# Windowed attention in a fused mixing kernel: the sums over v in eight tiles of 64 keys by 32 columns instead of four of 128 by 32, with two PSUM banks and an add on VectorE

## The chip, the cores and the metric

The kernel runs on one core of one Trainium2 chip. Its five engines are called by their short names in the profile: PE (TensorE, with PEld for its weight loads), DVE (VectorE), ACT (ScalarE), POOL (GpSimd) and SP (SyncE, which here only issues DMAs). The metric is the device time of one execution in microseconds; the time of a kernel is the median of its runs.

## The reference

All arrays are float32. `x` is 2048 tokens by 512 features. The output is a gated sum of two branches over the same `x`:

```
g = sigmoid((x * gate_w).sum(-1))
# branch A: Fourier mixing, the real part of a 2-D DFT, as four matrix products
a, b = x @ dft_hid_re.T, x @ dft_hid_im.T
A = dft_seq_re @ a - dft_seq_im @ b
# branch B: attention, 32 heads of 16 columns, causal, window of 256 keys
q, k, v = split(x @ wqkv)
scores = (q @ k.T) * 16 ** -0.5
scores = where(0 <= i - j < 256, scores, -1e9)
B = softmax(scores) @ v @ wo
out = g * A + (1 - g) * B
```

The change is in `softmax(scores) @ v`.

## The kernel before

Most of the work on PE is dense: the projections to q, k and v, the two hidden DFTs and the two sequence DFTs. Each float32 operand of a dense product is split into a high and a low part, and three products of the parts are summed. In the trace these are the tiles `d` (line 527, in two row halves of 64 partitions that run at the same time, `64*128`) and `dc` and `d` of lines 580 and 567 (whole array, `128*128`). The function `halves64` yields them step by step; a step is one matmul for the upper and one for the lower half.

The attention runs beside the dense work. The 32 heads are 8 groups of 4 heads, and the 2048 keys are 16 blocks of 128. The main loop (at the end of `fnet_window_mix`) counts `n` over 128 (group, key block) pairs, and each `n` has four quarter steps `q`. In quarters 0 and 2 stands `s_pair` (line 363, scores of 128 queries against up to 384 keys, two heads in the two row halves; DVE then takes the masked minimum, line 367). In quarters 1 and 3 stands `t_pair` (line 422, the same scores with keys on the partitions, for the pair nine blocks earlier; ACT takes the exponential into `pt`, line 425, and POOL zeroes the corners of the window, lines 427 and 431). After each of these `fill` puts in a few dense steps, as many as keep the dense work evenly spread. The whole order on PE, ACT, DVE, POOL and SP is written out by the program, and each engine works in that order.

Once for every 512 queries of a group, 32 times in all, `pv` (line 445) makes the sums of v. Call these the 32 blocks, numbered from 0; block `i` is group `i // 4` and quarter `c = i % 4` of the queries. It stands after quarter 3, behind the fill, so that the next instructions on PE are `s_pair`, fill, `t_pair`. For each key block it multiplies `pt` (128 keys by up to 384 queries) with the 32 columns of v of one head, and the four heads `j` take the four column tiles of the array (`128*32` in the trace). Column 16 of each 32 holds ones, so row 16 of a result is the sum of the weights. A quarter with `c > 0` takes six key blocks (1, 2, 3, 3, 2 and 1 blocks of 128 queries: 1536 columns for each head), a first quarter takes four (3, 3, 2, 1: 1152 columns). The operands are plain float32, and the trace has two matmuls, with two weight loads, for each one in the program.

The results of `s_pair`, `t_pair` and `pv` share a pool of PSUM, `ps_a`, with two buffers of two banks each. They go round: in 28 of the 32 blocks `pv` takes one buffer, the next `s_pair` the other, and the `t_pair` after it the buffer of `pv` again, for which ACT must have copied the sums out. (After block 27 that `t_pair` takes the other buffer, and the last three blocks have no `s_pair` behind them.) `pv` itself uses one bank of its buffer.

What follows a block is set off at fixed distances in quarter steps (the list `far`, line 1108): `o_evict` (line 454, ACT copies the 128 by 512 sums into one of three places of `ots`) after 1, `l_move` (the small DMA `lt<-ots` of the rows with the sums of weights, from SP's queue) after 4, then the reciprocal on DVE, its round trip through DRAM, and `o_mul` (line 475, POOL multiplies the sums by the reciprocals) after 28, and the store `o_scr<-ev` after 32. The next block comes 16 quarter steps after this one.

Of the kernel before, what the change touches and what calls it, by code (L numbers as in the profile page):

```python
# [7 lines left out]
F32 = mybir.dt.float32  # L8
# [6 lines left out]
P = 128  # L15
# [4 lines left out]
HG = 4  # L20
GROUPS = 8
NB = S // P
# [22 lines left out]
def fnet_window_mix(ctx: ExitStack, tc: tile.TileContext, xT, x, wqk, wv, wr, wi, cr, ci, wo, gw, out):  # L45
    nc = tc.nc
# [3 lines left out]
    st = ctx.enter_context(tc.tile_pool(name="st", bufs=4))  # L50
    ev = ctx.enter_context(tc.tile_pool(name="ev", bufs=EV))
    at = ctx.enter_context(tc.tile_pool(name="at", bufs=2))
    ps_a = ctx.enter_context(tc.tile_pool(name="ps_a", bufs=2, space=PSUM))
# [12 lines left out]
    def ld(dst, src):  # L66
        mark("sp", nc.sync.dma_start(dst, src))
# [11 lines left out]
    def mark(e, ins):  # L79
        last[e] = ins.ins  # L80
# [108 lines left out]
    with tc.manual_schedule(engines={mybir.EngineType.Activation, mybir.EngineType.DVE, mybir.EngineType.SP}):  # L189
# [11 lines left out]
        for dk in range(DK):  # L201
            c = slice(dk * 256, dk * 256 + 256)
# [29 lines left out]
    vt = [const.tile([P, 4, P], F32, name=f"vt{b}") for b in range(3)]  # L232
# [166 lines left out]
    PT = {}  # L399
# [34 lines left out]
    OT = {}  # L434
    ots = const.tile([P, 3, 512], F32, name="ots", tag="pt7")

    def pv(i):
        G, c = divmod(i, 4)
        o = ps_a.tile([P, 2, 512], F32, name="o", tag="st")[:, 0]
        kbs = range(max(0, 4 * c - 2), 4 * c + 4)  # L440
        for kb in kbs:
            a, e = max(kb, 4 * c), min(kb + 2, 4 * c + 3) + 1
            v = vt[(4 * G + kb // 4) % 3]
            for j in range(HG):
                nc.tensor.matmul(o[32 * j:32 * j + 32, (a - 4 * c) * P:(e - 4 * c) * P],  # L445
                                 v[:, kb % 4, 32 * j:32 * j + 32],
                                 PT[G * NB + kb][:, j, (a - kb) * P:(e - kb) * P],
                                 start=kb == kbs[0], stop=kb == kbs[-1], skip_group_check=True)
        OT[i] = o

    def o_evict(i):
        o = OT[i]
        OT[i] = ots[:, i % 3]
        nc.scalar.copy(OT[i], o)

    LT = {}

    def l_move(i):
        LT[i] = at.tile([P, 16], F32, name="lt")
        ld(LT[i], ots[:, i % 3][16:P:32])  # L460

    def l_turn(i):
        nc.vector.reciprocal(LT[i], LT[i])
# [625 lines left out]
    def at_time(t, fn, *args):  # L1089
        agenda.setdefault(t, []).append((fn, args))  # L1090
# [14 lines left out]
    for i in range(4 * GROUPS):  # L1105
        t = 4 * (VISIT * i + VISIT + LAG) + 3
        at_time(t + 0.5, pv, i)
        far = (1, 3, 9, 11, 16, 21, 24) if i == 4 * GROUPS - 1 else (1, 4, 11, 15, 21, 28, 32)
        for d, fn in zip(far, (o_evict, l_move, l_turn, l_inv, l_back, o_mul, o_out)):
            at_time(t + d, fn, i)  # L1110
        if i:
            at_time(t + 2, v_next, i + 2)
            at_time(t + 12, v_spread, i + 2)
# [73 lines left out]
```

## Time and profile before

| | |
|---|---|
| median of 3 runs | 849.21 us (847.05 to 849.4) |
| profiled execution, its own time | 850.56 us |
| its span | 848.9 us |
| mean granted clock of TensorE | 0.996 |
| PE busy | 821.5 us, 97% of the span |
| DVE, ACT, POOL busy | 63%, 49%, 43% |

A row of the groups by line reads: line, engine, operation, the tiles it writes and reads, shapes and count, then busy time in us (overlaps counted once) and the mean length of one in ns, then the idle time of its engine just before and what ended it. Matmuls overlap in the array, so the mean length of one is longer than the distance from one to the next. A row of the timeline has start and length in us, then engine, line and tiles; neighbours of one kind are merged into one row with a count.

### The profile page before, as it was taken

The page shows a single profiled execution, that of the slowest core. Times are in us where ns is not written, and L with a number is a line of the kernel's source. Part 1 is how long each engine was busy: PE and PEld are TensorE (multiplying, and loading weights), DVE is VectorE, ACT ScalarE, POOL GpSimd, SP SyncE. Part 2 cuts the span into 40 slices and gives each one's busy share as a digit, 9 for nine tenths or more (in the row PEclk, how much of TensorE's full clock was granted, in tenths as well). Part 3 has the DMA queues.
Part 4 walks back from the last instruction along what each step waited for, and adds up shares of the span by engine and source line. Part 5 has one row for each costly group of instructions (what it writes and reads, how often), then busy time and mean ns, then how long its engine had stood idle before and what let it go on. Part 6 is the DMA issues. An engine that isn't in the chain of part 4 may idle for free.

```text
span 848.9 us, 19774 instructions
## 1 busy us (share of the span) xinstructions
PE 821.5 (97%) x7298; PEld 654.2 (77%) x7298; DVE 531.1 (63%) x1504; ACT 418.0 (49%) x814; POOL 365.0 (43%) x683
## 2 busy tenths in 40 slices
PE   9999999998999899999999999899999999999998
PEld 7898777777777687777777777777777778788886
DVE  7276765555666678666657656676877536555553
ACT  6234655455555556555655656455555645222320
POOL 5002344433334336444444444454543546674540
PEclk9999999999999999999999999999999999999999
DMA  9865875558977546455646566787785567865531
GB/s 341 279 207 163 283 247 182 169 181 261 302 263 211 144 124 197 138 175 155 169 142 181 153 192 187 226 231 228 237 230 184 168 180 224 261 213 190 179 111 50
DMA packets 109344, 168.80 MB, mean 199 GB/s; under 512 B 34240, under 2 KB 43968, under 8 KB 109248
## 3 DMA queue, kind: packets, MB, share of 16 engines
q1 hardware_dynamic: 96192, 127.04, 48.4%
q0 software_dynamic: 11088, 39.33, 15.4%
q10 hardware_dynamic: 1968, 1.18, 0.5%
q8 instruction: 57, 0.93, 0.5%
q14 instruction: 39, 0.32, 0.1%
HBM read 107.74 MB, written 59.51 MB: 197 GB/s over the span
## 4 chain that ended last, share of the span: by engine, by line
PE 76%; DMA 8%; DVE 7%; issue 5%; ACT 3%; POOL 1%; SPq 1%; ACTq 0%; DVEq 0%; POOLq 0%
PE d L527 41%; PE o L445 9%; PE dc L580 8%; PE s L363 6%; PE t L1012 5%; PE t L422 4%; DVE junk L367 3%; PE d L567 3%; DMA ring<-qk_scr 2%; DMA raw<-ci 2%; ACT pt L425 1%; DVE lo L156 1%; DMA o_scr<-ev 1%; DVE big L140 1%; DMA stage<-ab_scr 1%
## 5 line engine op out<-in xcount | busy, mean ns | idle before, releaser
L367 DVE CUSTOM_DVE_ANT_0 junk<-s,mask 128x384 f32<-128x384 f32 (+2 forms) x512 | 271.9, 531 | 198.0 <-PE s L363 186.9
L527 PE MATMUL d<-big,hi 64*128 64x512 f32 x1920 | 344.5, 394 | 0.0
L427 POOL TENSOR_SCALAR_AFFINE_SELECT pt<-pt 128x256 f32<-128x256 f32 x256 | 112.3, 439 | 359.4 <-ACT pt L425 280.8
L425 ACT ACTIVATE pt<-t 128x768 f32<-128x768 f32 (+2 forms) x256 | 197.6, 772 | 123.8 <-PE t L422 121.4
L527 PEld LDWEIGHTS d<-big,hi 64*128 64x128 f32 x1920 | 195.5, 187 | 27.0 <-issue 0.6
L527 PE MATMUL d<-big,lo 64*128 64x512 f32 x960 | 206.2, 395 | 0.0
L527 PE MATMUL d<-hi,big 64*128 64x512 f32 x672 | 132.3, 392 | 0.0
L363 PE MATMUL s<-ring,ring 48*128 48x384 f32 (+2 forms) x512 | 99.5, 357 | 12.4 <-DMA ring<-qk_scr 3.7
L527 PEld LDWEIGHTS d<-big,lo 64*128 64x128 f32 x960 | 100.6, 187 | 13.2 <-issue 0.2
L155 ACT CAST hi<-raw 128x512 fp32r<-128x512 f32 x142 | 87.1, 618 | 30.0 <-PE d L527 15.2
L156 DVE TENSOR_TENSOR lo<-raw,hi 128x512 fp32r<-128x512 f32 x110 | 85.4, 777 | 12.9 <-ACT hi L155 12.9
L431 POOL TENSOR_SCALAR_AFFINE_SELECT pt<-pt 128x256 f32<-128x256 f32 x224 | 92.9, 415 | 0.0
L580 PE MATMUL dc<-big,hi 128*128 128x512 f32 x284 | 91.7, 392 | 0.0
L422 PE MATMUL t<-ring,ring 50*128 50x384 f32 (+2 forms) x512 | 87.8, 330 | 1.0 <-ACT pt L425 0.5
L445 PE MATMUL o<-pt,vt 128*32 128x384 f32 (+2 forms) x1408 | 84.3, 386 | 3.9 <-DVE ml L367 3.7
L527 PEld LDWEIGHTS d<-hi,big 64*128 64x128 f32 x672 | 76.8, 186 | 7.4
L363 PEld LDWEIGHTS s<-ring,ring 48*128 48x128 f32 x512 | 53.7, 185 | 37.3 <-issue 10.4
L527 PE MATMUL d<-lo,big 64*128 64x512 f32 x336 | 80.4, 392 | 0.0
L445 PEld LDWEIGHTS o<-pt,vt 128*32 128x32 f32 x1408 | 42.0, 110 | 49.7 <-issue 27.6
L422 PEld LDWEIGHTS t<-ring,ring 50*128 50x128 f32 x512 | 50.7, 185 | 14.5 <-ACT pt L425 2.1
L156 POOL TENSOR_TENSOR lo<-raw,hi 128x512 fp32r<-128x512 f32 x32 | 43.0, 1356 | 40.8 <-ACT hi L155 40.5
L580 PEld LDWEIGHTS dc<-big,hi 128*128 128x128 f32 x284 | 52.3, 188 | 8.7 <-issue 0.2
(123 smaller groups left out, 858.3 us busy)
## 6 DMA issues: line engine op xcount, KB each, us to landing
ring<-qk_scr SPq DMA_DIRECT2D x128, 192.0 KB
qk_scr<-home SPq DMA_DIRECT2D x32, 512.0 KB
raw<-cr POOLq DMA_DIRECT2D x32, 512.0 KB, 5.6
r_scr<-ev SPq DMA_DIRECT2D x44, 256.0 KB
raw<-ci POOLq DMA_DIRECT2D x18, 512.0 KB, 5.7
qk_scr<-home SPq DMA_DIRECT2D x32, 256.0 KB
ev<-l_scr SPq DMA_DIRECT2D x32, 256.0 KB
o_scr<-ev SPq DMA_DIRECT2D x32, 256.0 KB
```

The costliest lines, as they stand in the source:

```text
L155: jobs.append(lambda c=c: nc.scalar.copy(hi[:, c], raw[:, c]))
L156: jobs.append(lambda c=c: (nc.gpsimd if FIN else nc.vector).tensor_sub(lo[:, c], raw[:, c], f(hi[:, c])))
L363: nc.tensor.matmul(ps[:, h, :w], ring[0][r, p, j * P:j * P + P], ring[1][r, p, k0:k0 + w], start=True, stop=True)
L367: mark("dve", nc.vector.tensor_tensor_reduce(out=junk[:, :w], in0=ps[:, h, :w], in1=mask[:, WIN - w:], scale=1.0, scalar=3e38, op0=OP.add, ...
L422: nc.tensor.matmul(ps[:, h, :w], ring[1][r, p, q0:q0 + P], ring[0][r, p, q0:q0 + w], start=True, stop=True)
L425: nc.scalar.activation(pt[:, ph, :w], ps[:, :, :w], AF.Exp, scale=-1.0)
L427: nc.gpsimd.affine_select(a, a, pattern=[[0, 2], [1, P]], compare_op=OP.is_ge, fill=0.0, base=0, channel_multiplier=-1)
L431: nc.gpsimd.affine_select(a, a, pattern=[[0, 2], [-1, P]], compare_op=OP.is_gt, fill=0.0, base=0, channel_multiplier=1)
L445: nc.tensor.matmul(o[32 * j:32 * j + 32, (a - 4 * c) * P:(e - 4 * c) * P], v[:, kb % 4, 32 * j:32 * j + 32], PT[G * NB + kb][:, j, (a - kb ...
L527: nc.tensor.matmul(o.ps, lhs[r], rhs[r], start=start, stop=end and o.left == 0, skip_group_check=True)
L580: nc.tensor.matmul(ps, w[a][:, i % 8 * 128:i % 8 * 128 + 128], ab[SC[i]][:, b], start=i == ends[0] and a + b == 0, stop=i == ends[1] and a ...
L1012: nc.tensor.matmul(ps, o[:, a, c], fin(n, b, c), start=start and c == 0 and a + b == 0, stop=c == 1 and a == 1, skip_group_check=True)
```

## The change

`pv` now cuts each key block of 128 into its two halves of 64 keys. A half block of keys can only be seen by its own 320 queries, so its matmul is at most 320 columns long, and it is cut further at the edges of the quarter. The lower and the upper 64 partitions of the array work as two row tiles, so there are eight tiles of 64 by 32: two halves times four heads. Sums of the lower half go to the first bank of the buffer, those of the upper half to the second. The half blocks are put in pairs, one from each half, of equal length where that can be: for `c > 0` six pairs of 320, 320, 256, 192, 128 and 64 columns, 1280 in all; for a first quarter 320 with 384, 320 with 320, 256 with 192 and 128 with 64, which is 1024 columns in the lower and 960 in the upper half. The program has 1408 such matmuls in place of 704.

`o_evict` copies both banks (128 by 1024) with one ACT instruction: into place 0 or 1 of `ots` by the parity of the block, and into place 2. A new step `o_add`, two quarter steps after the block, adds place 2 to place 0 or 1 on DVE. `l_move` reads the added place. The rest of the chain keeps its distances.

```
-        o = ps_a.tile([P, 2, 512], F32, name="o", tag="st")[:, 0]
+        o = ps_a.tile([P, 2, 512], F32, name="o", tag="st")
...
-                nc.tensor.matmul(o[32 * j:32 * j + 32, (a - 4 * c) * P:(e - 4 * c) * P],
-                                 v[:, kb % 4, 32 * j:32 * j + 32],
-                                 PT[G * NB + kb][:, j, (a - kb) * P:(e - kb) * P],
-                                 start=kb == kbs[0], stop=kb == kbs[-1], skip_group_check=True)
+                spans[kb, h] = 0 if kb == 0 else max(k0, q0), min(k0 + 320, q0 + 512)
...
+        for n, pair in enumerate(pairs):
+            for h, (kb, _) in enumerate(pair):
+                a, e = spans[kb, h]
+                r = slice(64 * h, 64 * h + 64)
+                v = vt[(4 * G + kb // 4) % 3]
+                for j in range(HG):
+                    nc.tensor.matmul(o[32 * j:32 * j + 32, h, a - q0:e - q0], v[r, kb % 4, 32 * j:32 * j + 32],
+                                     PT[G * NB + kb][r, j, a - kb * P:e - kb * P],
+                                     start=n == 0, stop=n == len(pairs) - 1, skip_group_check=True)
...
-        OT[i] = ots[:, i % 3]
-        nc.scalar.copy(OT[i], o)
+        OT[i] = ots[:, i % 2]
+        nc.scalar.copy(ots[:, 0:3:2] if i % 2 == 0 else ots[:, 1:3], o)
+
+    def o_add(i):
+        nc.vector.tensor_add(OT[i], OT[i], ots[:, 2])
...
-        ld(LT[i], ots[:, i % 3][16:P:32])
+        ld(LT[i], OT[i][16:P:32])
...
-        far = (1, 3, 9, 11, 16, 21, 24) if i == 4 * GROUPS - 1 else (1, 4, 11, 15, 21, 28, 32)
-        for d, fn in zip(far, (o_evict, l_move, l_turn, l_inv, l_back, o_mul, o_out)):
+        far = (1, 2, 3, 9, 11, 16, 21, 24) if i == 4 * GROUPS - 1 else (1, 2, 4, 11, 15, 21, 28, 32)
+        for d, fn in zip(far, (o_evict, o_add, l_move, l_turn, l_inv, l_back, o_mul, o_out)):
```

On PE, block 2 (group 0, third quarter) stands in the program before the change as these rows; `o` are the sums, `pt` the six key blocks in the order they are taken, `vt` the v of three quarters, `s` the score pair that follows, and the last number is the four heads:

```order
L445 MATMUL o_1928<-pt_1447,vt1_303 32x128 x4
L445 MATMUL o_1928<-pt_1513,vt1_303 32x256 x4
L445 MATMUL o_1928<-pt_1575,vt2_304 32x384 x4
L445 MATMUL o_1928<-pt_1670,vt2_304 32x384 x4
L445 MATMUL o_1928<-pt_1740,vt2_304 32x256 x4
L445 MATMUL o_1928<-pt_1805,vt2_304 32x128 x4
L363 MATMUL s_1953<-ring1_286,ring0_285 128x384 x2
```

The same block after the change; `x8` are the lower and the upper half of one key block, four heads each, and a row of `x4` is one half:

```order
L457 MATMUL o_1970<-pt_1592,vt2_304 32x320 x8
L457 MATMUL o_1970<-pt_1711,vt2_304 32x320 x8
L457 MATMUL o_1970<-pt_1782,vt2_304 32x256 x4
L457 MATMUL o_1970<-pt_1530,vt1_303 32x256 x4
L457 MATMUL o_1970<-pt_1530,vt1_303 32x192 x4
L457 MATMUL o_1970<-pt_1782,vt2_304 32x192 x4
L457 MATMUL o_1970<-pt_1847,vt2_304 32x128 x4
L457 MATMUL o_1970<-pt_1464,vt1_303 32x128 x4
L457 MATMUL o_1970<-pt_1464,vt1_303 32x64 x4
L457 MATMUL o_1970<-pt_1847,vt2_304 32x64 x4
L363 MATMUL s_2019<-ring1_286,ring0_285 128x384 x2
```

The middle key blocks now come first and the oldest last, and two halves stand side by side in each pair; the neighbours of the block are the same as before. Between the `s` pair and the next `t` pair stand three dense steps in 13 of the blocks (all eight first quarters, and blocks 3, 7, 17, 21 and 25) and four in the other 16 that have an `s` pair, before and after the change alike.

On DVE, behind the first block, the difference reads as follows; `junk,ml<-s` are the masked minima of a score pair:

```order
 L367 ISA junk,ml<-s,mask 128x384 [waits DVE_49]
 L367 ISA ml 128x1
+L468 TENSOR_TENSOR ots<-ots 128x512 [waits Activation_49]
 L367 ISA junk,ml<-s,mask 128x384 [waits DVE_49,PE_49]
 L367 ISA ml 128x1
```

The add stands behind the minima of the `s` pair that follows the block and ahead of those of the next one. On ACT the copy keeps its place and grows from 128x512 to 128x1024. On SP the DMA `lt<-ots` keeps its place and waits for DVE where it waited for ACT.

More of the change, by code (lines that the diff above doesn't have):

```diff
@@ L438, in pv @@
         G, c = divmod(i, 4)
-        o = ps_a.tile([P, 2, 512], F32, name="o", tag="st")[:, 0]
[L440 to L445, printed above, removed]
-                                 v[:, kb % 4, 32 * j:32 * j + 32],
-                                 PT[G * NB + kb][:, j, (a - kb) * P:(e - kb) * P],
-                                 start=kb == kbs[0], stop=kb == kbs[-1], skip_group_check=True)
+        o = ps_a.tile([P, 2, 512], F32, name="o", tag="st")
+        q0 = 4 * c * P
+        spans = {}
+        for kb in range(max(0, 4 * c - 2), 4 * c + 4):
+            for h in range(2):
+                k0 = kb * P + 64 * h
+                spans[kb, h] = 0 if kb == 0 else max(k0, q0), min(k0 + 320, q0 + 512)
+        pairs = [((kb, 0), (kb, 1)) for kb in range(4 * c, 4 * c + 4)]
+        if c:
+            pairs[2:] = [((kb, h), (8 * c + 1 - kb, 1 - h)) if h == 0 else ((8 * c + 1 - kb, 1 - h), (kb, h))
+                         for kb in (4 * c + 2, 4 * c + 3) for h in range(2)]
+        for n, pair in enumerate(pairs):
[7 more added lines that the diff above has]
+                                     start=n == 0, stop=n == len(pairs) - 1, skip_group_check=True)
         OT[i] = o
```

## Prediction

> **What bounds the kernel now.** I read the page's shares first, then the groups by line and shape, then the timeline around single blocks of `pv`, and last the waits.
>
> ```profile
> PE 821.5 (97%) x7298; PEld 654.2 (77%) x7298; DVE 531.1 (63%) x1504; ACT 418.0 (49%) x814; POOL 365.0 (43%) x683
> ```
>
> PE is busy for 97% of 848.9 us and works in the program's order, so what is taken from PE comes off the end, unless PE then waits. A block of `pv` and what follows, first with four dense steps behind it (block 2: PE, then ACT):
>
> ```profile
> 129.11 0.43 PE L527 MATMUL d<-hi,big 64*128 64x512 f32 x2
> 129.46 2.80 PE L445 MATMUL o<-pt,vt 128*32 128x128 f32 x48
> 132.19 0.45 PE L363 MATMUL s<-ring,ring 48*128 48x384 f32 x2
> ...
> 132.71 0.62 PE L527 MATMUL d<-hi,big 64*128 64x512 f32 x4
> ...
> 133.40 0.34 PE L422 MATMUL t<-ring,ring 50*128 50x384 f32 x2
> ```
> ```profile
> 132.33 0.59 ACT L454 COPY ots<-o 128x512 f32<-128x512 f32 x1 [2.59 <-PE o L445]
> ```
>
> then block 7 with three (PE, its weight loads, ACT), and the length of a first quarter (block 8):
>
> ```profile
> 234.20 0.44 PE L363 MATMUL s<-ring,ring 48*128 48x384 f32 x2
> ...
> 235.18 0.34 PE L422 MATMUL t<-ring,ring 50*128 50x384 f32 x2
> ```
> ```profile
> 235.03 0.19 PEld L422 LDWEIGHTS t<-ring,ring 50*128 50x128 f32 x2
> ```
> ```profile
> 234.39 0.59 ACT L454 COPY ots<-o 128x512 f32<-128x512 f32 x1 [2.60 <-PE o L445]
> ```
> ```profile
> 252.50 2.15 PE L445 MATMUL o<-pt,vt 128*32 128x384 f32 x32
> 254.58 0.45 PE L363 MATMUL s<-ring,ring 48*128 48x384 f32 x2
> ```
>
> The reader is to see two things. A block costs PE 2.73 us to the start of the next `s` pair (132.19 - 129.46), a first quarter 2.08. And the `t` pair takes the buffer that the sums have just left: in block 7 ACT's copy ends at 234.98, the weights of `t` load at 235.03 and its matmul starts at 235.18. That is right behind the copy. So PE does not wait much there now, but nothing is left over either. In block 2 the copy ends at 132.92 and `t` starts 0.48 later, because a fourth dense step stands between. Some other four-step blocks sit a little closer, as block 14 does (375.85 to 376.29, 0.44):
>
> ```profile
> 375.26 0.59 ACT L454 COPY ots<-o 128x512 f32<-128x512 f32 x1 [2.20 <-PE o L445]
> ```
> ```profile
> 376.29 0.34 PE L422 MATMUL t<-ring,ring 50*128 50x384 f32 x2
> ```
>
> **Step 1, the columns on PE: 9.9 us less.** From 1152 to 1536 columns in two passes a block grows by 0.65 us, so a column costs 0.65 / 768 = 0.85 ns a pass. If the two row halves run side by side, a block with `c > 0` has 1280 columns in place of 1536 and saves 2 x 256 x 0.85 = 0.43 us. Two things are given back. The last pair has 64 columns, 0.054 us a pass, but a weight load takes 110 ns on average, and that for the second of the two passes starts only as the first pass does:
>
> ```profile
> L445 PEld LDWEIGHTS o<-pt,vt 128*32 128x32 f32 x1408 | 42.0, 110 | 49.7 <-issue 27.6 <-DVE ml L367 7.3 <-POOL pt L431 5.0
> ```
> ```profile
> 130.46 0.13 PEld L445 LDWEIGHTS o<-pt,vt 128*32 128x32 f32 x4 [0.19 <-issue]
> ```
>
> So one pass lasts 0.11, 0.055 longer. Four loads take 0.13 where one takes 0.11, so a tile starts about 7 ns behind the one before it, and four more tiles cost 0.03. That leaves 0.35. A first quarter has 1024 columns in its longer half, 128 less: 0.22 - 0.03 = 0.19. Sum: 24 x 0.35 + 8 x 0.19 = 9.9 us; with nothing given back it would be 12.1.
>
> The Trainium skill, page "TensorE: Matmul & The Clock Gate", section "LDWEIGHTS (loading the stationary operand)", puts a load at its columns divided by 1.2, in ns, an estimate of 27 ns for 32 columns; by that the short passes would not be held and step 1 would be 1.3 us larger. The row above has 110 ns from start to end, and no run here shows a pass of 64 columns. I stay with the row.
>
> **Step 2, the longer copy: 8.5 us more.** ACT now copies 1024 elements a partition in one instruction. Its price comes from the same engine's rows for other lengths out of PSUM:
>
> ```profile
> L425 ACT ACTIVATE pt<-t 128x768 f32<-128x768 f32 x224 | 181.9, 812 | 106.8 <-PE t L422 104.5 <-PE d L527 0.6 <-POOL pt L431 0.4
> ...
> L454 ACT COPY ots<-o 128x512 f32<-128x512 f32 x32 | 18.8, 586 | 79.7 <-PE o L445 66.2 <-issue 13.5
> ...
> L425 ACT ACTIVATE pt<-t 128x512 f32<-128x512 f32 x16 | 9.6, 598 | 5.2 <-PE t L422 5.1
> ```
>
> 812 - 598 = 214 ns for 256 elements, so 512 more cost 0.43 us and the copy takes 1.02. It ends 0.43 later after the end of the sums, and so does the release of the buffer. In the 13 blocks with three dense steps all of this falls on PE, since `t` stood right behind the copy: 13 x 0.43 = 5.6 us. With four steps `t` stands 0.44 to 0.48 behind and needs 0.20 (block 7), so 0.24 to 0.28 is covered and 0.15 to 0.19 is not: 15 blocks x 0.19 = 2.9. Block 27, whose `t` takes the other buffer, and the last three, with no `s` pair and so a tile more in between, lose nothing. What is late next is ACT's following work, but with 49% busy and gaps of 2.6 us before the copies it has room. Bounds: 13 x 0.43 alone, 5.6, and 0.43 in all 28 blocks, 12.0.
>
> Steps 1 and 2 nearly cancel: from the start of a block to its `t` pair PE takes 0.35 less for the sums and waits 0.2 or 0.43 more for the buffer.
>
> **Step 3, the add on DVE: 1.0 us more.** The nearest row is a subtraction of the same shape out of SBUF:
>
> ```profile
> L156 DVE TENSOR_TENSOR lo<-raw,hi 128x512 fp32r<-128x512 f32 x110 | 85.4, 777 | 12.9 <-ACT hi L155 12.9
> ```
>
> 32 x 0.78 = 25 us on an engine that is busy for 531 of 849. The add stands behind the two minima of the `s` pair, which end at 133.84 in block 2, after the copy; what is queued behind it is the next minimum, at 134.66:
>
> ```profile
> 133.76 0.08 DVE L367 DVE_READ_ACCUMULATOR2_ANT ml<- 128x1 f32 x1
> 134.66 0.56 DVE L367 CUSTOM_DVE_ANT_0 junk<-s,mask 128x384 f32<-128x384 f32 x1 [0.82 <-PE s L363]
> ```
>
> It just fits into that gap of 0.82. Later DVE is fuller (9.83 of 10 us from 600 to 610), and there PE already waits for the minima:
>
> ```profile
> 600.00:610.00 10.00, 9.63 (x86) 7.37 (x84) 9.83 (x27) 7.01 (x12) 7.27 (x14) 1.00 0.72 230
> ```
> ```profile
> PE o L445 <- DVE ml L367: 3.7, 6, 0.9
> ...
> PE s L363 <- DVE ml L367: 2.7, 7, 0.7
> ```
>
> Five blocks lie between 549 and 640. The cost lies between 0 and 5 x 0.78 = 3.9 us; I take 1.0, near the low end, since the add falls into the stretch where DVE has just idled for want of scores.
>
> **Step 4, the queues: 0.3 us more.** On SP `lt<-ots` now waits for the add, with the stores and loads of the queue behind it:
>
> ```profile
> 132.94 0.60 SPq L67 DMA_DIRECT2D lt<-ots  x1
> 135.17 0.33 SPq L67 DMA_DIRECT2D ab_scr<-ev  x1
> ```
>
> The add would end about 134.6 and the issue 0.6 later, so the next entry is hardly late. ACT's copies, with the exponentials of `t` queued behind them, now reuse a place of `ots` after two blocks and wait for POOL's product of the block before last. The tightest is block 9's copy behind the product of block 7, which ends at 273.39, 0.35 ahead:
>
> ```profile
> 272.11 1.28 POOL L475 TENSOR_TENSOR ev<-ots,ev 128x512 f32<-128x512 f32 x1 [4.21 <-DMA ev<-l_scr]
> ```
> ```profile
> 273.74 0.59 ACT L454 COPY ots<-o 128x512 f32<-128x512 f32 x1 [2.16 <-PE o L445]
> ```
>
> That is one place; 0 to 1 us. POOL's corners of the window, now wanted earlier in the block, cost nothing: the newest key block now comes in the fifth of six pairs and not last, and the loads' 5.0 us behind POOL in the row of step 1 are no idle time of PE, whose one listed wait at `o` is that for DVE.
>
> **Sum.** -9.9 + 8.5 + 1.0 + 0.3 = -0.1 us. The profiled execution took 850.56, which is 1.35 above the median of 849.21; on the scale of the median I forecast 849.1 us. About 0.3%, 2.5 us, is what a measurement of this kernel can tell from no change.
>
> **Rivals.**
>
> *The halves lag (slower).* Each matmul of the program runs as two passes. If the upper half of a head may begin only once the second pass of the lower half has begun, the halves run one pass apart, and each shorter pair waits for the longer one before it. With passes of 0.27, 0.27, 0.22, 0.16, 0.11 and 0.11 us in the order lower, lower, upper, upper, the last pass starts 2.43 us after the first and the block saves 0.1 in place of 0.35, a first quarter nothing. Then -2.4 + 8.5 + 1.3 = +7.4: 856.6 us. It decides once a block is still longer than about 2.45 us to its `s` pair. Against it: the dense halves do run side by side (four of them in 0.62 us at 132.71), and the four column tiles start without waiting for each other's second pass, if 24 loads in 0.81 us are read so. For it: nothing in this trace has two passes and two row halves at once. The Trainium skill, same page, part 3, section "The mechanism", says that matmuls start and end strictly in program order, only weight loads being pulled ahead; that points to this rival, and the trace, which does not tell heads and passes apart, cannot settle it. Chance 0.17.
>
> *The halves do not overlap at all,* so the change does not do what it says: 2560 columns, 1024 x 2 x 0.85 = 1.7 us more for each of 24 blocks, 1.4 (832 columns) for the other 8, 53 us; with steps 2 to 4 some 912. The dense halves speak against it. Chance 0.03.
>
> *A cheaper entrance (faster).* Before a block PE changes from `64*128` to `128*32`: the row at 129.11 is 0.43 long for two matmuls of 0.39, so the second dense half starts at 129.15; dense steps stand 0.23 apart (0.62 for two steps at 132.71), so the next could start at 129.37 or 129.38, but the block starts at 129.46. If tiles of 64 rows on both sides spare these 0.09 us at most, 32 blocks give 2.9, and if steps 3 and 4 cost nothing, 1.3 more: 844.9. At the exit nothing can be won, since there `t` waits for the copy. Against it: nothing here shows that the rows and not the columns cause the loss. Chance 0.10.
>
> **From this to the numbers.** The forecast has 0.70, with a range of its own of 846 to 852.5 from step 2 (-2.9 to +3.5) and step 3 (-1 to +2.9): 0.07 of it below 846.6, 0.10 above 851.8. Faster: 0.07 + 0.09 = 0.16. Slower: 0.10 + 0.17 + 0.03 = 0.30. Same: 0.54. The range runs from 845.0 to 857.0; it leaves out the total failure, the low side of the third rival and part of the lag.
>
> **What would show it.** Right: sums of a block at 2.35 to 2.4 us to the `s` pair (first quarters 1.9), copies of 1.02 us, `t` 0.2 behind every copy with weight loads of `t` idle for 0.2 to 0.45 before, PE's busy time down by some 10 us and its idle time up by as much. Wrong: blocks near 2.6, or `t` waits that do not grow, or DVE waits at `s` and `o` that double.

## The result, and the profile after

The changed kernel takes 852.45 us (median of 13 runs, 849.84 to 859.31), the kernel before 848.55 in the same comparison (13 runs, 844.80 to 853.19). The ratio is 1.0055, with a 95% interval from 1.0031 to 1.0078: the change costs 0.55%, 4.7 us (the two medians alone differ by 3.9). The forecast was 849.1 and no measurable difference.

The profiled execution took 850.24 us, which is near the fast end of the thirteen. Its page, and the groups of the lines that changed:

```profile
PE 819.4 (97%) x8706; PEld 664.1 (78%) x8706; DVE 548.2 (65%) x1536; ACT 431.4 (51%) x814; POOL 367.2 (43%) x683
```
```profile
L457 PE MATMUL o<-pt,vt 64*32 64x320 f32 (+4 forms) x2816 | 74.2, 348 | 3.6 <-DVE ml L367 3.6
L457 PEld LDWEIGHTS o<-pt,vt 64*32 64x32 f32 x2816 | 54.0, 106 | 30.0 <-issue 10.2 <-POOL pt L431 5.3
L422 PEld LDWEIGHTS t<-ring,ring 50*128 50x128 f32 x512 | 50.1, 185 | 28.3 <-ACT ots L465 11.4 <-ACT pt L425 3.4 <-ACT tick L544 2.6
L465 ACT COPY ots<-o 128x1024 f32<-128x1024 f32 x32 | 32.4, 1014 | 70.3 <-PE o L457 41.4 <-issue 24.2 <-PE s L363 2.9
L468 DVE TENSOR_TENSOR ots<-ots 128x512 f32<-128x512 f32 x32 | 22.2, 693 | 6.2 <-ACT ots L465 6.2
```

Block 2 again, as in the prediction: TensorE (PE), its weight loads, ScalarE, VectorE, and SyncE's queue.

```profile
129.50 2.45 PE L457 MATMUL o<-pt,vt 64*32 64x320 f32 x96
131.88 0.45 PE L363 MATMUL s<-ring,ring 48*128 48x384 f32 x2
...
133.14 0.45 PE L422 MATMUL t<-ring,ring 50*128 50x384 f32 x2
```
```profile
133.13 0.19 PEld L422 LDWEIGHTS t<-ring,ring 50*128 50x128 f32 x2 [0.31 <-ACT ots L465]
```
```profile
132.07 1.02 ACT L465 COPY ots<-o 128x1024 f32<-128x1024 f32 x1 [2.30 <-issue]
```
```profile
133.45 0.69 DVE L468 TENSOR_TENSOR ots<-ots 128x512 f32<-128x512 f32 x1
```
```profile
134.17 0.59 SPq L67 DMA_DIRECT2D lt<-ots  x1
```

The sums and the copy are as forecast: 2.38 us to the `s` pair (131.88 - 129.50) where it was 2.73, and a copy of 1.02. The `t` pair is not. It starts at 133.14, 0.05 behind the end of the copy (133.09), where the prediction took from block 7 that it needs 0.20. Block 7 itself, after the change, shows the same (233.26 + 1.02 to 234.33):

```profile
233.26 1.02 ACT L465 COPY ots<-o 128x1024 f32<-128x1024 f32 x1 [2.26 <-PE o L457]
```
```profile
234.33 0.44 PE L422 MATMUL t<-ring,ring 50*128 50x384 f32 x2
```

So the longer copy costs TensorE less than forecast. From the first matmul of a block to its `t` pair (to the next matmul where no `t` pair follows) the 32 blocks take 109.7 us in all in this trace, and 114.8 in the trace of before: 5.1 less, where steps 1 and 2 together had 1.4. Nevertheless PE's busy time is only 2.1 us down and its idle time 1.7 up (27.4 to 29.1), where the prediction's sign of being right was some 10 for each.

One thing stands out only in the last row of block 2. The move of the row sums, `lt<-ots`, starts 1.08 us behind the end of the copy; before, it started 0.02 behind it (132.92 to 132.94). SyncE's waits show the same over the whole kernel, first before, then after:

```profile
SPq L67 <- ACT ots L454: 18.3, 12, 2.8
...
SPq L67 <- DVE ml L367: 9.4, 11, 2.3
```
```profile
SPq L67 <- DVE ml L367: 33.6, 21, 5.4
SPq L67 <- DVE ots L468: 33.5, 15, 4.0
```

And the trace itself shows no loss: a span of 848.5 us against 848.9. The loss is seen only over all timed executions. Their granted clock gives a first hint: 0.9947 in the mean over the thirteen, where 98 runs of the kernel before in five later comparisons have 0.9970 to 0.9979. At 849 us a thousandth of the clock is 0.85 us, so some 2.2 of the 4.7 us are clock.

### The profile page after: what moved, and what is told of

Its sections match the earlier page's. It is cut to its first block, busy times and chain, and to the rows that moved or that the text cites. A ratio compares the mean times of both kernels' runs of the same rounds, so it can differ in the third digit from the quotient of the medians.

```text
span 848.5 us, 22652 instructions
## 1 busy us (share of the span) xinstructions
PE 819.4 (97%) x8706; PEld 664.1 (78%) x8706; DVE 548.2 (65%) x1536; ACT 431.4 (51%) x814; POOL 367.2 (43%) x683
## 4 chain that ended last, share of the span: by engine, by line
PE 66%; DMA 12%; DVE 8%; issue 5%; ACT 5%; POOL 2%; SPq 1%; DVEq 0%; ACTq 0%; POOLq 0%
PE d L541 35%; PE dc L594 8%; DMA ring<-qk_scr 6%; PE o L457 6%; PE t L1026 5%; PE s L363 5%; PE t L422 4%; DVE junk L367 3%; PE d L581 3%; DMA raw<-ci 2%; ACT pt L425 2%; ACT ots L465 1%; SPq L67 1%; DMA stage<-ab_scr 1%; DVE big L140 1%
## 5 line engine op out<-in xcount | busy, mean ns | idle before, releaser
L427 POOL TENSOR_SCALAR_AFFINE_SELECT pt<-pt 128x256 f32<-128x256 f32 x256 | 112.9, 441 | 357.2 <-ACT pt L425 284.4
L422 PE MATMUL t<-ring,ring 50*128 50x384 f32 (+2 forms) x512 | 90.3, 341 | 5.1 <-ACT pt L425 1.4
L431 POOL TENSOR_SCALAR_AFFINE_SELECT pt<-pt 128x256 f32<-128x256 f32 x224 | 94.7, 423 | 0.0
L457 PE MATMUL o<-pt,vt 64*32 64x320 f32 (+4 forms) x2816 | 74.2, 348 | 3.6 <-DVE ml L367 3.6
L457 PEld LDWEIGHTS o<-pt,vt 64*32 64x32 f32 x2816 | 54.0, 106 | 30.0 <-issue 10.2
L465 ACT COPY ots<-o 128x1024 f32<-128x1024 f32 x32 | 32.4, 1014 | 70.3 <-PE o L457 41.4
```

The lines of the kernel that those rows point to most:

```text
L422: nc.tensor.matmul(ps[:, h, :w], ring[1][r, p, q0:q0 + P], ring[0][r, p, q0:q0 + w], start=True, stop=True)
L427: nc.gpsimd.affine_select(a, a, pattern=[[0, 2], [1, P]], compare_op=OP.is_ge, fill=0.0, base=0, channel_multiplier=-1)
L431: nc.gpsimd.affine_select(a, a, pattern=[[0, 2], [-1, P]], compare_op=OP.is_gt, fill=0.0, base=0, channel_multiplier=1)
L457: nc.tensor.matmul(o[32 * j:32 * j + 32, h, a - q0:e - q0], v[r, kb % 4, 32 * j:32 * j + 32], PT[G * NB + kb][r, j, a - kb * P:e - kb * P] ...
```

## The experiments

Theories, as the expectations name them. **A**: the longer copy costs more than step 2 said. **B**: the addition and the queues cost more than steps 3 and 4 said; its two forms are **V**, VectorE's time, and **W**, SyncE's wait for the addition and the transfers behind it. **C**: the loss is not in the blocks but in waits on ring loads and in the clock. **T**: what the blocks gain is lost at the tail. The tail is the stretch behind the attention, where TensorE works through the rest of the sequence DFT (`dc`) and the output products (`t<-fin,ring`); these wait for `ex`, an operand that ScalarE copies, in its order behind the `hi` part of a freshly loaded `raw`. All ratios are to the kernel before on the same chip, from five rounds. The kernels of one set below ran on one chip, each set on another, and the changed kernel itself came out differently in two comparisons (1.0055 above, 1.0097 in e5), so parts are best compared within a set.

### First set: the parts one by one

**e1**, the kernel before, unchanged. 

> The kernel before, unchanged, so that its scatter, its granted clock and a second profile of it are known. All theories: a ratio of 1.000 with an interval of about 0.002 to either side. Theory A (the blocks themselves: the longer copies cost more than the 8.5 us of step 2) needs nothing of it. Theory C (the loss is not in the blocks but in how often TensorE waits on a ring load or runs at a granted clock of half speed): the mean clock of its runs is 0.997 or above, against the mean of 0.995 of the changed kernel's thirteen runs, and its second profile shows no more TensorE idle time than the first (23 us).

Measured: 0.9995 (0.9976 to 1.0014), clock 0.9979 in the mean. Its traced execution, 850.26 us, is the slowest of its twelve runs (844.79 to 850.26), whereas that of the changed kernel was the second fastest of thirteen. So traces of the two, set side by side, hide a few us of the difference.

**e2**, the changed kernel without the addition.

```
     def o_add(i):
-        nc.vector.tensor_add(OT[i], OT[i], ots[:, 2])
+        pass
```

> The changed kernel without the addition on VectorE; the sums of the upper half blocks of keys are left out, and the move of the row sums waits for ScalarE's copy again. Theory A (the longer copies): no gain, 1.005 of the kernel before. Theory B (steps 3 and 4: the additions, some 1 us each on VectorE, delay the minima or the move of the row sums delays the loads behind it on SyncE): the 4.7 us of loss go, 1.000 or below. Theory C (retimed ring loads and clock): 1.002 to 1.005, with a mean clock near that of the changed kernel.

Measured: 1.0034 (1.0009 to 1.0058), clock 0.9943. Between B and A: without the addition some 2 us less than 1.0055 (of another comparison, and the intervals overlap), but a loss stays.

**e3**, e2 with a copy of one bank: step 1 by itself.

```
-        nc.scalar.copy(ots[:, 0:3:2] if i % 2 == 0 else ots[:, 1:3], o)
+        nc.scalar.copy(OT[i], o[:, 0])
```

> The changed kernel with a copy of the first bank alone (128x512, as before the change) and no addition; the sums of the upper half blocks of keys are left out. This is step 1 by itself: the eight tiles without the longer copy. Forecast by step 1: 9.9 us below the kernel before, a ratio of 0.988, with t pairs that no longer wait for the copy. Theory A (step 1 was right and step 2 too small): 0.988. Rival A2 (step 1 was too large: the shorter blocks are given back by the next wait, on a ring load, on VectorE's minima or on the t pair): 0.993 to 0.997. Theory C: 0.990 to 0.995, with a lower clock than the kernel before.

Measured: 0.9995 (0.9968 to 1.0023), clock 0.9938. Forecast by step 1 was 0.988. Without the longer copy and the addition, the eight tiles still win no measurable time. That is the main finding, and its trace shows where much of the gain goes. The first dense step of the tail, in the kernel before and in e3:

```profile
700.46 0.74 PE L580 MATMUL dc<-big,hi 128*128 128x512 f32 x2
```
```profile
690.68 0.73 PE L594 MATMUL dc<-big,hi 128*128 128x512 f32 x2
```

9.8 us early, 3.4 of which are clock: before had two stretches at half clock by then, which cost 1.7 us each, e3 none. Then e3 at the tail's first output products (PE, and windows of 2 us with the granted clock in the third column from the end), and the chain of waits that leads there:

```profile
714.40 0.88 PE L1026 MATMUL t<-fin,ring 128*128 128x256 f32 x6
720.38 0.99 PE L1026 MATMUL t<-fin,ring 128*128 128x256 f32 x6 [4.41 <-ACT ex L140]
```
```profile
718.00:720.00 2.00, 0.00 (x0) 0.00 (x0) 0.00 (x0) 0.57 (x2) 2.00 (x2) 1.00 0.36 120
720.00:722.00 2.00, 1.62 (x8) 1.46 (x9) 0.50 (x2) 1.38 (x4) 1.51 (x2) 0.80 0.54 127
722.00:724.00 2.00, 2.00 (x9) 1.89 (x8) 0.44 (x2) 0.08 (x1) 1.73 (x3) 0.50 0.80 263
724.00:726.00 2.00, 2.00 (x11) 1.69 (x11) 0.71 (x2) 0.00 (x0) 1.92 (x3) 0.85 0.90 297
```
```profile
676.81 6.76 DMA o_scr<-ev
...
683.60 6.14 DMA ev<-l_scr
...
689.92 1.37 POOL ev L489
...
691.31 7.47 DMA o_scr<-ev
...
698.85 7.34 DMA raw<-ci
...
706.26 0.63 ACT hi L155
...
706.96 2.56 POOL lo L156 x2
...
709.54 9.79 DMA raw<-ci
...
719.43 0.62 ACT hi L155
720.05 0.28 ACT ex L140
```

TensorE waits 4.41 us there (before: 1.6, in e1 1.8), and then runs at half the clock for 3.4 us, another 1.7 lost. From 683.6 on the chain is transfers of 6 to 10 us one behind the other, through SyncE's queue (`raw<-ci` waits behind the store `o_scr<-ev`) and the two raw buffers; no matmul is in it. The trace of before has the same row, from its store to the product:

```profile
698.35 7.53 DMA o_scr<-ev
...
727.40 0.98 PE t L1012 x6
```

It is as long there, 29.05 us against 29.07. But in e3 the store started only 7.0 us earlier than before (691.31), not 9.8: POOL's product ahead of it waited for the load `ev<-l_scr`, and that for the store before it. The wait is longer by that difference. Of the 9.8 us, 5.5 are left at the end of the trace (spans of 843.4 and 848.9).

**e4**, the kernel before with the doubled copy alone.

```
-        OT[i] = ots[:, i % 3]
-        nc.scalar.copy(OT[i], o)
+        OT[i] = ots[:, i % 2]
+        nc.scalar.copy(ots[:, 0:3:2] if i % 2 == 0 else ots[:, 1:3], o.unsqueeze(1).to_broadcast([P, 2, 512]))
...
```

> The kernel before with ScalarE's copy doubled alone: the one bank of sums is read twice and written to two places (128x1024 out of one 512-column bank), the places taken in turns of two as in the changed kernel, no addition. This is step 2 by itself, on blocks of the old length. Forecast by step 2: 8.5 us above the kernel before, 1.010 (bounds 5.6 to 12.0 us: 1.0066 to 1.014). Theory A (step 2 too small): 1.015 or more. Theory B and theory C: 1.010 or less.

Measured: 1.0100 (1.0078 to 1.0122), 8.5 us. A falls. The total is just what step 2 was priced at, but the trace puts it elsewhere, so the match is luck in part. In the 32 blocks the longer copy costs 4.2 us and not 8.5 (119.0 against 114.8): 0.27 in a block with three dense steps and 0.04 in one with four, since `t` starts 0.05 behind the copy. And at the tail, though nothing was saved ahead of it, TensorE waits 4.0 us for `ex`, where it waited 1.6, and then works at half the clock from 730 to 736.8 us:

```profile
PE t L1012 <- ACT ex L140: 4.0, 1, 4.0
```

### Second set: is it the tail?

**e5**, the changed kernel again. 

> The changed kernel again, for a second profile and the scatter on this chip. All theories: 1.0055 within its interval (1.003 to 1.008), mean clock 0.994 to 0.995. Theory T (the tail: what the blocks gain is lost at the first output products, which wait for ScalarE's last piece of ex at the end of a row of DMAs of fixed length): that wait is 1.8 us or more, and the clock is halved behind it. Theory C (ring loads): waits of over 1 us on ring<-qk_scr stand again at two or more places between 190 and 640 us.

Measured: 1.0097 (1.0082 to 1.0112), above the expected interval; clock 0.9953. The wait for `ex` is 3.4 us, with a halved clock behind it (T); in the first trace of the changed kernel it is 1.7, hardly more than before. Waits of over 1 us on `ring<-qk_scr` stand at three places (1.3 us at 199, 1.9 at 282, 2.2 at 538), so C holds too. One of these, and the windows around it:

```profile
PE s L363 <- DMA ring<-qk_scr: 1.9, 1, 1.9
```
```profile
282.00:284.00 2.00, 0.34 (x4) 0.38 (x6) 0.00 (x0) 0.00 (x0) 0.34 (x1) 1.00 0.72 217
284.00:286.00 2.00, 2.00 (x17) 2.00 (x15) 1.13 (x4) 0.97 (x2) 0.08 (x1) 0.74 0.18 71
286.00:288.00 2.00, 2.00 (x14) 2.00 (x12) 0.88 (x3) 0.74 (x2) 0.68 (x2) 0.50 0.04 17
```

**e6, e7, e8**: the tail's output products 16 dense steps later, in e3, in the changed kernel and in the kernel before.

```
-                after(b + 3 * k, wo_product, i, k)
-            after(b + 36, wo_store, i)
+                after(b + 16 + 3 * k, wo_product, i, k)
+            after(b + 44, wo_store, i)
```

> The kernel with eight tiles, a copy of the first bank alone and no addition (the sums of the upper half blocks of keys are left out), and the output products of the tail 16 dense steps (16 of 0.227 us, 3.6 us) later, their operands prepared when they were. Theory T: the wait of 4.4 us on ex goes to under 1 us, and with it one halving of the clock (1.7 us): 4 to 5 us below the kernel with one bank, 0.994 to 0.995 of the kernel before, clock up by 0.002. Theory C (the loss lies in the ring loads and in the attention's part): no gain, 0.999 to 1.000.

> The changed kernel with the output products of the tail 16 dense steps later. Theory T: 3 to 4 us below the changed kernel, 1.001 to 1.002 of the kernel before. Theory C: no gain, 1.005.

> The kernel before with the output products of the tail 16 dense steps later. In its two profiles the second product waited 1.6 and 1.8 us, with a halved clock behind one of the two. Theory T: a gain of 1.5 to 2.5 us, 0.997 to 0.998, so that the changed kernel stays behind it by 3 to 4 us when both have the later products. Theory C: 1.000.

Measured: 1.0151 (1.0127 to 1.0174), 1.0230 (1.0206 to 1.0255), 1.0177 (1.0158 to 1.0196). All slower, and a bad test: the products now meet VectorE while it works on the next pair's operands, as e8's waits from 700 us on show:

```profile
PE t L1012 <- DVE rt L1017: 14.0, 13, 2.0
```

What they still say: among themselves the three stand in the same order as their originals (against e8, e6 is 2.2 us faster, where e3 was 0.4 faster than before; e7 is 4.5 slower, where the changed kernel was 4.7, and 8.2 in e5 on this chip).

### Third set: the addition alone, and the tail moved as a whole

**e9**, the kernel before with the addition alone (of a tile of zeros, with the places of `ots` taken in turns of two, as in the changed kernel).

```
+        nc.vector.tensor_add(OT[i], OT[i], ots[:, 2])
...
-        ld(LT[i], ots[:, i % 3][16:P:32])
+        ld(LT[i], OT[i][16:P:32])
```

> The kernel before with the addition alone: after ScalarE's copy of the one bank, VectorE adds a tile of zeros to it, and the move of the row sums waits for VectorE, at the same places in the order as in the changed kernel. This is steps 3 and 4 without steps 1 and 2. Forecast by steps 3 and 4: 1.3 us, 1.0015 (bounds 0 to 4). Theory B (the addition and the wait on it cost what is missing): 1.004 or more. Theory T with the clock (the loss is in waits of over 1.5 us, on ring loads and at the tail's second output product, each of them followed by 3.4 us at half the clock): 1.000 to 1.002, mean clock as the kernel before (0.997 to 0.998).

Measured: 1.0063 (1.0037 to 1.0088), 5.3 us where steps 3 and 4 had 1.3; clock 0.9955 against 0.9974 of the kernel before in that set. B. The traced execution, the fastest of its runs, does not show the price (its blocks and its way to the tail are no longer than before), but it shows what changed, in SyncE's queue:

```profile
SPq L67 <- DVE ml L367: 37.9, 21, 5.5
SPq L67 <- DVE ots L458: 36.4, 15, 4.1
```

**e10, e11**: all of the tail's output work 6 dense steps later, in e3 and in the kernel before.

```
-FIRST_OUT, PAIR = 104, 38
+FIRST_OUT, PAIR = 110, 38
```

> The eight tiles with a copy of the first bank alone and no addition (the sums of the upper half blocks of keys are left out), and all of the tail's output work, loads, sums, splits and products, 6 dense steps (1.4 us) later, so that its parts keep their distances, which the run with 16 steps broke (there TensorE waited 0.4 to 2 us for VectorE at a dozen products). Theory T: the wait for ex falls from 4.4 to about 3 us, 0.997 to 0.999. Rival: the row of loads moves with the output work, and nothing is gained, 1.000 or above.

> The kernel before with all of the tail's output work 6 dense steps later. Theory T: its wait of 1.6 to 1.8 us for ex falls to about 0.4, the halved clock behind it goes, 0.997 to 0.998. Rival: the row of loads moves with the output work, 1.000 or above.

Measured: e10 0.9962 (0.9937 to 0.9986), e11 0.9978 (0.9955 to 1.0000), with a clock of 0.9988. The ratios are those that T forecast, within intervals of 0.002 to 0.003 to either side. In e11's trace the wait for `ex` is short, and the clock stays up (728 to 732 us: 1.00):

```profile
PE t L1012 <- ACT ex L140: 0.5, 1, 0.5
```

In e10 it is still 3.4. So with the same tail the eight tiles with one bank win 0.0016 over the four, 1.4 us of 9.9, and that is within the noise of the two.

**e12**, the changed kernel with the copy shared by ScalarE and VectorE.

```
-        nc.scalar.copy(ots[:, 0:3:2] if i % 2 == 0 else ots[:, 1:3], o)
+        nc.scalar.copy(OT[i], o[:, 0])
+        nc.vector.tensor_copy(ots[:, 2], o[:, 1])
```

> The changed kernel with the longer copy shared: ScalarE copies the first bank (128x512) and VectorE the second beside it, then the addition as before. It computes the reference. Step 2 is taken away, and VectorE gets a copy more in each block (32 times some 0.6 us). By the profiles' busy time in the attention, step 2 was 3.5 us: theory of the blocks: 1.000 to 1.003. Rival (VectorE's extra copy delays the minima by as much as it saves): 1.005 or above. Theory T: whatever the blocks gain, a mean clock of 0.994 to 0.995 stays.

Measured: 1.0164 (1.0136 to 1.0191), worse than the rival said. The wait has moved from ScalarE to VectorE, whose copy stands in its queue behind other work, and the 32 blocks take 121.4 us in all, 11.7 more than in the changed kernel's trace:

```profile
PE t L422 <- DVE ml L367: 12.8, 29, 0.6
```

### Fourth and fifth set (e13 to e16, e17 and e18): what in the addition costs

**e13**, e9 with the addition on the spare tile, so that nobody waits for it.

```
-        nc.vector.tensor_add(OT[i], OT[i], ots[:, 2])
+        nc.vector.tensor_add(ots[:, 2], ots[:, 2], ots[:, 2])
```

> As the run with the addition alone, but the addition works on the spare tile of zeros, so that VectorE spends the same time at the same place and nobody waits for it: the move of the row sums waits for ScalarE's copy again. Theory W (the cost is the wait of the move on SyncE, and the row of transfers behind it): 1.000 to 1.002. Theory V (the cost is VectorE's time): 1.005 or more.

Measured: 1.0036 (1.0017 to 1.0056), clock 0.9968. Between the two theories: VectorE's time alone costs about 3 us. e9's 1.0063 is from another chip and the intervals overlap, so what the wait adds is not shown by this pair.

**e14**, the changed kernel with the row sums of both halves moved by two transfers and added afterwards, the large addition later; **e15**, the changed kernel with the tail 6 steps later; **e16**, both.

```
     def l_move(i):
...
-        ld(LT[i], OT[i][16:P:32])
+        for h, part in enumerate((OT[i], ots[:, 2])):
+            ld(LT[i][:, h], part[16:P:32])
...
     def l_turn(i):
+        nc.vector.tensor_add(LT[i][:, 0], LT[i][:, 0], LT[i][:, 1])
...
-        for d, fn in zip(far, (o_evict, o_add, l_move, l_turn, l_inv, l_back, o_mul, o_out)):
+        far = (1, 3, 8, 9, 11, 16, 21, 24) if i == 4 * GROUPS - 1 else (1, 4, 8, 11, 15, 21, 28, 32)
+        for d, fn in zip(far, (o_evict, l_move, o_add, l_turn, l_inv, l_back, o_mul, o_out)):
```

> The changed kernel with the row sums of both halves moved by two transfers as soon as ScalarE's copy is done and added in VectorE's short form (128x16) ahead of the reciprocal; the addition of 128x512 stands later, where nothing waits for it. It computes the reference. SyncE issues one transfer more in each block. Theory W: 2 to 4 us below the changed kernel, 1.000 to 1.003. Theory V: 1.005 or above.

> The changed kernel with all of the tail's output work 6 dense steps later, as was done to the kernel before (0.9978) and to the eight tiles with one bank (0.9962, against 0.9995 without). Theory T: 2 to 3 us below the changed kernel, 1.002 to 1.003; it stays behind the kernel before with the later tail by 4 us.

> Both: the row sums moved without the wait for the addition, and the tail's output work 6 dense steps later. Theories W and T together: 0.996 to 1.000. Theory V: 1.002 to 1.003, as the later tail alone.

Measured: e14 1.0266 (1.0231 to 1.0301), e15 1.0035 (1.0012 to 1.0059), e16 1.0302 (1.0274 to 1.0330). e15 is near T's 1.002 to 1.003, and against e11, of another set, the changed kernel stays 0.0057 behind with the same tail, about as without. But not by T's way: in e15's trace the wait for `ex` is 4.5 us, longer than in the two traces of the changed kernel with the earlier tail (1.7 and 3.4). e14 misses by 20 us, through a wait of its own making: the addition writes a place that the transfer still reads, so VectorE waits for the transfer, with its minima behind it.

```profile
DVE ots L468 <- DMA lt<-ots: 22.5, 10, 5.2
```

**e17, e18**: the changed kernel with the move one and a half quarters of a key block later, behind the next entry of SyncE's queue (e18 with the later tail).

```
-        far = (1, 2, 3, 9, 11, 16, 21, 24) if i == 4 * GROUPS - 1 else (1, 2, 4, 11, 15, 21, 28, 32)
+        far = (1, 2, 3, 9, 11, 16, 21, 24) if i == 4 * GROUPS - 1 else (1, 2, 4 if i > 27 else 5.5, 11, 15, 21, 28, 32)
```

> The changed kernel with the move of the row sums one and a half quarters of a key block later in the order, behind the load of the inverse sums of the block before (but for the last four blocks). Theory W (SyncE's wait for the addition is a part of the loss): SyncE's waits for the addition fall from 33.5 us to under 15, and the time by 1.5 to 2.5 us, 1.002 to 1.004. Rival: the move is now late for the reciprocal, and VectorE waits for it, 1.006 or above.

> The same, and the tail's output work 6 dense steps later. Theories W and T: 1.000 to 1.002. Rival: 1.004 or above.

Measured: 1.0178 (1.0150 to 1.0205) and 1.0169 (1.0136 to 1.0203): the rival, and stronger. e17's waits of SyncE for the addition fall to 25.7 us only, and VectorE, where the reciprocal of the row sums stands in line with the minima, now waits for them:

```profile
DVE lt L477 <- DMA lt<-ots: 20.1, 11, 6.0
```

One of the eleven, with what it does to TensorE (PE's row) and to the clock:

```profile
229.59 0.25 DVE L477 RECIPROCAL lt<-lt 128x16 f32<-128x16 f32 x1 [3.52 <-DMA lt<-ots]
```
```profile
230.44 0.79 PE L541 MATMUL d<-big,hi 64*128 64x512 f32 x2 [3.17 <-DVE home L109]
```
```profile
230.00:232.00 2.00, 1.56 (x8) 1.36 (x10) 2.00 (x4) 0.37 (x1) 1.75 (x3) 0.50 0.41 158
```

The move's start behind the end of the copy, as a mean over the 32 blocks of each trace, is 0.97 us before, 1.63 after, 2.04 in e9 and 2.34 in e17. From 1.63 to 2.34 the kernel loses another 7 to 10 us (1.0178 against 1.0097 and 1.0055) and its clock falls to 0.9857. This suggests that the row of move, landing, reciprocal has little left over, and that the addition takes 0.7 to 1.1 us of it. The mean alone does not decide: in e12's trace it is 2.74, and the reciprocal waits there only once, for 1.1 us.

None of these beats the kernel before but e10, which leaves work out, and e11, which computes all: the kernel before with its tail 6 dense steps later, 0.9978, with an interval that just reaches 1.

## Why the prediction was wrong

The time is 4.7 us above a sum that came to nothing, and the sum hid errors in several terms. Two readings of the traces tell them apart. One is the time of the 32 blocks, from the first matmul of the sums to the `t` pair behind (or to the next matmul). The other is the first tail step's start, less 1.7 us for each halving of the clock ahead of it: what the parts do within the whole attention. In e4 and e15 one halving is at the very start and not in the recorded clock (see the end).

| kernel | starts, us | halvings | net | net, to before | blocks, us | blocks, to before |
|---|---|---|---|---|---|---|
| before (profile, e1, e8, e11) | 700.5, 698.7, 698.5, 700.4 | 2, 1, 1, 1 | 697.1, 697.0, 696.8, 698.7 | 0 | 114.8 | 0 |
| step 1 (e3, e6, e10) | 690.7, 688.3, 692.6 | 0, 0, 2 | 690.7, 688.3, 689.2 | -8.0 | 104.5 | -10.3 |
| steps 1, 2 (e2) | 695.6 | 1 | 693.9 | -3.5 | 109.8 | -5.0 |
| step 2 (e4) | 702.2 | 1 | 700.5 | +3.1 | 119.0 | +4.2 |
| steps 3, 4 (e9) | 696.9 | 0 | 696.9 | -0.5 | 114.8 | 0 |
| all (profile, e5, e7, e15) | 698.0, 699.5, 699.1, 696.1 | 1, 2, 0, 1 | 696.3, 696.1, 699.1, 694.4 | -0.9 | 109.8 | -5.1 |

Block times of one kernel agree within 0.3 us. The net starts of one kernel differ by up to 4.7, so a single one says little.

- **Step 1, -9.9.** Its size is right where it was priced: blocks of 2.38 us, all eight tiles side by side, 10.3 us less in the blocks and 8.0 to the start of the tail. (One part of its working is wrong and small: the second pass of 64 columns starts 0.06 us behind the first and not 0.11, so the weight load does not hold it.) The step of the argument that failed stands in the first part: what is taken from PE comes off the end, "unless PE then waits". PE then waits: 4.4 us in place of 1.6 at the second output product in e3, with a halved clock behind it. Timed, step 1 is worth 0.4 us (2.7 gained to 2.0 lost), with a later tail 1.4. Of the 8.0 us the longer wait takes 2.8, and the lower mean clock of e3's runs (0.9938 against 0.9972 of the kernel before in that set) another 2.9; the 2.3 that this leaves lie inside the interval. The wait stood in the profile of before, as 1.6 us, and was not priced. What makes it longer is shown for e3 alone, where the row of transfers did not come forward as far as the tail did. It is not the saving in every case: the wait is 4.0 in e4 and 3.0 in e9, which save nothing, and the same row from store to product took from 28.9 us (the changed kernel) to 30.5 (e4).
- **Step 2, +8.5.** Timed alone, 8.5 (6.6 to 10.4), but as said under e4 this is luck in part. The term was mis-sized in the blocks: 4.2 us alone and 5.3 on top of step 1 (e2 against e3, 109.8 against 104.4). The prediction let `t` start 0.20 behind the copy, because it stood there in block 7; where the copy holds it, it starts 0.05 behind. Timed on top of step 1 the longer copy costs 3.3 (1.0034 against 0.9995, within noise of about 3). The timed terms don't add: -0.4, +8.5 and +5.3 make 13.4, and 4.7 was measured. Why they don't is not shown; that the copy fills time which PE would otherwise wait away at the tail is not borne out, since e2 waits there for 4.1 us and e3 for 4.4.
- **Steps 3 and 4, +1.0 and +0.3.** Too small: alone 5.3 us (3.1 to 7.5), where the bounds were 0 to 3.9 for the addition and 0 to 1 for the queues. VectorE's time alone came to 3.1 (1.4 to 4.8, e13). Step 4 looked at the entry behind `lt<-ots` in SyncE's queue and found it hardly late; it did not follow the row sums on to the reciprocal on VectorE, which is in line with the minima. e17 shows that a later move makes VectorE wait there. In the traces of the changed kernel and of e9 the reciprocal waits not at all or once for 0.5 us, so that it is what costs the timed executions their time is argued, not shown.
- **What the sum left out.** In the changed kernel some 4 us of the 5.1 that the blocks gain are gone before the tail starts (a mean of four traces that differ by 4.7). They are lost between the blocks, for which the sum had only the 1.3 us of steps 3 and 4; no single wait ahead of the tail is longer than 2.2 us in the profile and e5.
- **The rivals.** The halves neither lag nor exclude each other: 2.38 us and not 2.6, and first quarters of 1.86 where the lag had 2.08. The Trainium skill, page "TensorE: Matmul & The Clock Gate", part 3, "The mechanism", has matmuls start and end in program order, which pointed to the lag; 96 matmuls of two row halves and two passes each in 2.45 us do not show that lag. The trace does not tell passes apart, so whether the order itself holds stays open. A cheaper entrance is not seen either: from the last dense step to the first matmul of a block it is 0.32 us (median) before and after. The kernel did end slower, but by a way that none of the rivals had.
- **The scale.** The sum was made against one traced execution of 850.56 us, near the slow end of its kind (thirteen runs have a median of 848.55; e1's own trace is the slowest of its twelve), while the traced execution of the changed kernel lies near the fast end. So the two traces, 848.9 and 848.5 us, hide the loss.

What stays open: in which places the timed executions lose the 2.5 us of 4.7 that are not clock and that no trace shows, where the halvings of the untraced runs lie, and how the 5.3 us of the addition divide between VectorE and SyncE.

## What to carry to other kernels

An engine that is 97% busy is the bound only as far as the next chain of fixed length: follow a saving to the last instruction, and price the waits that stand there already, since the row of transfers that ends in such a wait need not come forward with the saving. A small operation put between a copy and a transfer is priced not only at its own engine but also at the end of the row that the transfer begins, up to the in-order queue where its result is awaited. Take one trace for one sample: time each part alone before the terms are added, and do not expect their times to add. And a term is not confirmed by its total: look whether the time stands in the place where it was priced.

## What the runs showed of the hardware

- **The clock halves after a half-idle stretch.** In a single execution the halvings start on a grid of 3.41 us (within 0.03), and its phase differs from one execution to the next. Over the 20 traces, from 15 us on, a stretch of the grid at full clock in which PE was idle for 1.83 us or more was each time followed by at least 3.41 us at half clock, one with under 1.5 never, and between these both happened (1.61 us of idling in the stretch from 724 us of the kernel before did not, 1.52 in that from 558 us of the changed kernel did). So a wait of 2 us inside one stretch costs 3.7: itself and half of the next 3.41. The Trainium skill, page "TensorE: Matmul & The Clock Gate", part 1, "What's actually happening", has the clock fall after an idle window of some 3.4 us; the length agrees, but here about half a window of idling was enough.
- **The recorded clock can miss one.** Two of the first matmuls take 1.19 us together in e4 (first row), 0.70 in e1 (second row), and the first `s` pair starts 1.7 us later (37.27 against 35.58, and 37.26 in e15), with a granted clock of 1.00 in that window:

```profile
6.02 1.19 PE L293 MATMUL s<-big,hi 128*128 128x512 f32 x2 [0.57 <-ACT hi L206]
```
```profile
6.02 0.70 PE L293 MATMUL s<-big,hi 128*128 128x512 f32 x2 [0.57 <-DVE hi L208]
```
- **Eight tiles run at once in two passes.** 96 matmuls of 64 rows by 32 columns start and end within 2.45 us; 48 of 128 rows took 2.80.
- **A matmul starts right behind the copy that frees its buffer.** In e4 and in the changed kernel `t` starts 0.05 to 0.06 us behind the end of ScalarE's copy of 1.01 us in all 28 blocks where it takes the buffer of the sums.
